# A fused Fourier mixing and feed-forward kernel: transform split 49 by 64 instead of 56 by 56, its first stage on 64x64 tiles of TensorE

## The chip, the cores and the metric

One NeuronCore of one Trainium2 chip runs the whole kernel. The metric is the device time of one execution in microseconds. Times and profiles come from the chip; a profile is one execution taken by the hardware profiler.

## The reference

Two parts follow each other. The first is a Fourier transform over the sequence of 3136, a complex 256 by 256 mixing with bias and a soft threshold, and the inverse transform. The second is a gated feed-forward part with a convolution of three taps.

```python
batch, seq, dim = (8, 3136, 256); d_ff = 1024
X = np.fft.rfft(x, axis=1)
Yr = Xr @ w_r - Xi @ w_i + b_r
Yi = Xr @ w_i + Xi @ w_r + b_i
Yr = np.sign(Yr) * np.maximum(np.abs(Yr) - 0.01, 0.0)      # Yi likewise
y = np.fft.irfft(Yr + 1j * Yi, n=3136, axis=1)
h = np.maximum(y @ w_in, 0.0)
for k in range(3):                                # hp: h with a row of zeros at both ends
    conv_out += conv_w[k][None, None, :] * hp[:, k:k + S, :]
out = h * (1.0 / (1.0 + np.exp(-conv_out))) @ w_out
```

## The kernel before

The transform of length 3136 = 56 x 56 is done in two matmul steps with twiddle factors in the second step's table, and back in two more. Through the middle the data passes twice through DRAM, as `sc1` (after the first step) and `sc2` (after the third).

- **Stage one** (`stage1`, and `stage1_head` for batch 0): a call takes four columns `j` of one batch (`JC = 4`), loads them as `xr` (112 rows: 56 points of two halves), and multiplies with the block-diagonal table `f1` in two plain fp32 matmuls 112x112 by 512 columns. ScalarE copies each result (`ps_s`, one PSUM bank) to `a1`, and one DMA stores it to `sc1`. A batch takes 7 calls; 56 in all.
- **Stage two** (`stage2`): an *item* is one batch and one group of four lines `u` (`UG = 4`, `NG = 7` groups a batch, 56 items). `load_a2` gathers 112 x 4 x 256 from `sc1`; eight plain fp32 matmuls with 128 streamed columns (the table `t2`) put the spectrum, transposed, into `ps_s2`. ScalarE and VectorE split it into a high and a low fp32r part (`fh`, `fl`).
- **Mix** (`mix`): 36 fp32r matmuls of 256 columns into three banks `ps_mx0` to `ps_mx2`. VectorE adds the bias (`p1`, two operations), forms `v` in four operations, and thresholds it with `r` from ScalarE; `sh` and `sl` are its high and low parts, `sl` by GpSimd.
- **Stage three** (`stage3`): 12 fp32r matmuls with the tables `i1_hi`, `i1_lo` into `ps_s3` (two banks), one copy `z1` by ScalarE, one store to `sc2`.
- **Stage four** (`stage4`): inverse first step. A piece loads `z2` from `sc2` and uses its 128-column slices as the stationary operand; the table `i2` (112 columns) streams. Eight plain fp32 matmuls a piece, `NPC = 7` pieces a batch. The result `yh`, `yl` stays in SBUF.
- **Feed-forward** (`up`, `down`): 12 fp32r matmuls of 450 columns and 21 of 256 for each of 224 steps, with the pieces of stage four of a later batch between them.

Plain fp32 matmuls stand in a profile as two records each. The weights of the feed-forward part arrive as float64 bits and are converted by VectorE and ScalarE in the background (`later`), a few operations per item, from the item 3 on.

The order within each engine is set by the Tile scheduler, from the order of the code and its own estimates. In the code the loop over `it` loads `a2` two items ahead, does stage two of item `it`, mix of `it - 1`, stage three of `it - 3`, and calls of stage one as far ahead as the `while` condition lets it. All DMAs are issued on SyncE's queue. The PSUM banks of this part are one for `ps1` (stage one), two for `ps2`, three for `psm`, two for `psa`.

## Time and profile before

| what | value |
|---|---|
| median of 3 runs (lowest, highest) | 1770.43 us (1767.99, 1770.92) |
| the profiled execution | 1769.05 us, span 1767.3 us |
| granted TensorE clock in it | 0.995 |
| TensorE busy | 1731.0 us (98%), 12096 matmul records |
| VectorE busy | 1524.3 us (86%) |
| ScalarE busy | 1229.1 us (70%) |
| GpSimd busy | 134.7 us (8%) |
| DMA | 164.63 MB, mean 93 GB/s |

The share of busy time is a mean over the transform (about the first third) and the feed-forward part, and these have different limits; stretches of the span have to be read apart. The ends of matmul records are modelled, so the distance from one start to the next says what a matmul costs. A line such as L245 names the line of the kernel's code.

### The profile page before, as it was taken

The numbers are of one execution on the slowest core, as the hardware profiler recorded it, in microseconds if no ns is written. First come the engines' busy times: TensorE is split into PE (matmuls) and PEld (weight loads), VectorE is DVE, ScalarE is ACT, GpSimd is POOL, SyncE is SP. The second block draws the span as 40 slices with busy tenths as digits, with TensorE's granted clock in tenths as the row PEclk, the third lists the DMA queues.
The fourth block names the chain that finished last, engine by engine and source line by source line (L and its number), as shares of the span: only waits on it lengthen the run. The fifth ranks groups of instructions, "written<-read, shape, count | busy, mean of one in ns | idle before, by whom it ended". The sixth has DMA issues, their size and how long they took to land.

```text
span 1767.3 us, 29387 instructions
## 1 busy us (share of the span) xinstructions
PE 1731.0 (98%) x12096; PEld 1621.6 (92%) x12096; DVE 1524.3 (86%) x1820; ACT 1229.1 (70%) x1590; POOL 134.7 (8%) x60
## 2 busy tenths in 40 slices
PE   6899999999998999999999999999999999999999
PEld 2788888888998999999999999999999999999998
DVE  2899999998896988988888888888888888888887
ACT  2667777776665777777777777777777777777766
POOL 0122222222232000000000000000000000000000
PEclk8999999999999999999999999999999999999999
DMA  9777677677534110111111011111101111100001
GB/s 263 216 230 236 196 232 216 192 230 228 164 111 136 43 43 22 32 53 53 32 53 53 22 55 51 49 46 52 43 22 43 53 43 43 42 22 22 22 22 42
DMA packets 107382, 164.63 MB, mean 93 GB/s; under 512 B 8816, under 2 KB 86000, under 8 KB 107248
## 3 DMA queue, kind: packets, MB, share of 16 engines
q1 hardware_dynamic: 107248, 162.74, 30.9%
q8 instruction: 96, 1.57, 0.4%
q14 instruction: 38, 0.31, 0.1%
HBM read 85.65 MB, written 77.07 MB: 92 GB/s over the span
## 4 chain that ended last, share of the span: by engine, by line
PE 93%; DMA 3%; DVE 1%; ACT 1%; issue 0%; SPq 0%; ACTq 0%
PE acc L470 31%; PE ps_h L442 31%; PE ps_mx L304 12%; PE ps_s L423 5%; PE ps_s L280 5%; PE ps_s L331 4%; PE ps_s L245 4%; DMA i_raw<-in_inv_dram 2%; DMA z<-sc 1%; DMA sc<-ha 0%; DMA a<-sc 0%; DMA sc<-a 0%; ACT a L246 0%; DVE cw L212 0%; DVE yl L430 0%
## 5 line engine op out<-in xcount | busy, mean ns | idle before, releaser
L470 PE MATMUL acc<-wout,gh 128*128 128x256 f32 x3136 | 567.0, 280 | 0.0
L451 DVE SCALAR_TENSOR_TENSOR c<-h,cw,c 128x896 f32<-128x896 f32 x448 | 513.1, 1147 | 47.3 <-ACT c L449 46.3
L442 PE MATMUL ps_h<-yh,win 128*128 128x450 f32 x1792 | 551.0, 368 | 0.1
L470 PEld LDWEIGHTS acc<-wout,gh 128*128 128x128 f32 x3136 | 493.7, 188 | 6.5
L470 PE MATMUL acc<-wout,gl 128*128 128x256 f32 x1568 | 437.6, 281 | 0.0
L444 ACT ACTIVATE h<-ps_h 128x900 f32<-128x900 f32 x224 | 207.7, 927 | 254.8 <-PE ps_h L442 254.8
L442 PEld LDWEIGHTS ps_h<-yh,win 128*128 128x128 f32 x1792 | 338.7, 189 | 26.4 <-DVE yl L430 0.8
L442 PE MATMUL ps_h<-yl,win 128*128 128x450 f32 x896 | 329.2, 367 | 0.0
L470 PEld LDWEIGHTS acc<-wout,gl 128*128 128x128 f32 x1568 | 293.7, 188 | 0.1
L457 DVE TENSOR_TENSOR gl<-c,gh 128x896 fp32r<-128x896 f32 x224 | 243.1, 1089 | 53.6 <-ACT gh L456 50.1
L453 DVE TENSOR_TENSOR c<-h,c 128x896 f32<-128x896 f32 x224 | 243.6, 1088 | 46.9 <-ACT c L452 46.7
L456 ACT CAST gh<-c 128x896 fp32r<-128x896 f32 x224 | 209.8, 942 | 49.4 <-DVE c L453 49.4
L452 ACT ACTIVATE c<-c 128x896 f32<-128x896 f32 x224 | 213.3, 952 | 23.9 <-DVE c L451 21.0
L304 PE MATMUL ps_mx<-wmix_lo,fh 128*128 128x256 f32 x672 | 202.2, 301 | 0.0
L304 PE MATMUL ps_mx<-wmix_hi,fh 128*128 128x256 f32 x672 | 196.9, 294 | 0.5 <-DVE v L313 0.3
L304 PE MATMUL ps_mx<-wmix_hi,fl 128*128 128x256 f32 x672 | 188.7, 282 | 1.3 <-DVE fl L288 1.2
L442 PEld LDWEIGHTS ps_h<-yl,win 128*128 128x128 f32 x896 | 168.9, 189 | 11.0
L449 ACT ACTIVATE c<-h,cw 128x896 f32<-128x896 f32 x168 | 175.5, 1044 | 2.6 <-DVE gl L457 0.2
L321 POOL TENSOR_TENSOR sl<-v,sh 128x1024 fp32r<-128x1024 f32 x56 | 134.5, 2402 | 423.1 <-PE ps_s L331 300.0
L313 DVE TENSOR_TENSOR v<-ps_mx,p 64x512 f32<-64x512 f32 x224 | 154.0, 688 | 3.3
L304 PEld LDWEIGHTS ps_mx<-wmix_lo,fh 128*128 128x128 f32 x672 | 126.4, 188 | 12.3 <-issue 12.3
L304 PEld LDWEIGHTS ps_mx<-wmix_hi,fl 128*128 128x128 f32 x672 | 126.0, 188 | 11.8 <-issue 9.9
(84 smaller groups left out, 2023.0 us busy)
## 6 DMA issues: line engine op xcount, KB each, us to landing
a<-sc SPq DMA_DIRECT2D x56, 448.0 KB, 5.0
sc<-z SPq DMA_DIRECT2D x56, 448.0 KB, 3.3
z<-sc SPq DMA_DIRECT2D x56, 448.0 KB, 3.8
xr<-in_x_dram SPq DMA_DIRECT2D x55, 448.0 KB, 4.7
out_dram<-o SPq DMA_DIRECT2D x27, 896.0 KB, 4.0
sc<-a SPq DMA_DIRECT2D x49, 448.0 KB, 4.9
sc<-ha SPq DMA_DIRECT2D x7, 448.0 KB, 7.5
win_bits<-in_moe_w_in_dram SPq DMA_DIRECT2D x4, 512.0 KB, 7.6
```

Of the source, the lines that this page charges most:

```text
L304: nc.tensor.matmul(ps[c][:, k, :], lt, rh, start=(n == 0), stop=(n == len(mm) - 1))
L313: nc.vector.tensor_tensor(v[dst, :, k, :], ps[c][src], p1[src, c], op=ALU.add)
L321: SL_ENG.tensor_tensor(sl, v, sh.bitcast(F32), op=ALU.subtract)
L442: nc.tensor.matmul(ps[:, a, 0:CH + 2], lt, rh, start=(n == 0), stop=(n == len(mm) - 1))
L444: nc.scalar.activation(h, ps[:, :, 0:CH + 2], AF.Relu)
L449: nc.scalar.mul(c, h[:, :, 0:CH], cw[:, 0, f:f + 1])
L451: nc.vector.scalar_tensor_tensor(c, h[:, :, k:k + CH], cw[:, k, f:f + 1], c, op0=ALU.mult, op1=ALU.add)
L452: nc.scalar.activation(c, c, AF.Sigmoid)
L453: nc.vector.tensor_tensor(c, h[:, :, 1:CH + 1], c, op=ALU.mult)
L456: nc.scalar.copy(gh, c)
L457: nc.vector.tensor_tensor(gl, c, gh.bitcast(F32), op=ALU.subtract)
L470: nc.tensor.matmul(acc[m // 2][:, m % 2, :], lt[:, sl], rh[:, f, :], start=(f == 0 and n == 0 and m % 2 == 0), stop=(f == NF - 1 and n == ...
```

## The change

The length is split as 49 x 64 instead of 56 x 56. In the first step 49 points give 25 lines `u` (0 to 24; 1 to 24 complex, 0 real), in the second step 64 points give 64 lines of the spectrum.

- **Items.** Lines 1 to 24 are six groups of four per batch. Line 0 of four batches is gathered into one item of its own, twice: 50 items instead of 56. Such an item loads four pieces of 64 rows and stores four pieces.
- **Stage one.** A call again takes four columns `j`, of 64 half-columns (`H = 32`), so a batch takes 8 calls. The two halves lie at partitions 0 to 48 and 64 to 112. `quarters` issues four matmuls with 49 rows and 64 output columns of the array each, streaming 512 columns: two halves times two pairs of columns, each with tile size 64x64 and its own corner of the array. The two halves write two banks. Two loads and two stores a call instead of one and one.
- **Stage three** writes in two halves of two lines, through a single bank, with a copy each. `ps1` now has two banks and `psa` one.
- **Mix.** The two additions of the bias become one of 1024 elements that reads `ps[2]` twice; `r` lies in the memory of `p1`; `sl` has two buffers.
- **Stage four.** `z2` has 100 rows, the streamed table 98 columns; 8 pieces a batch.
- The `while` condition of stage one lets it run ahead by other numbers.

```diff
-R = 56
-U = 28
-SL = 57
+R = 49
+R2 = 64
+U = 24
 SP = 64
-H = 28
+H = 32
...
+NQ = H // 4
...
-        ps1 = ab.enter_context(tc.tile_pool(name="ps1", bufs=1, space=PSUM))
+        ps1 = ab.enter_context(tc.tile_pool(name="ps1", bufs=2, space=PSUM))
...
+        def load_x(pool, b, jc, **kw):
+
+            xr = pool.tile([P, JC, D], F32, name="xr", **kw)
+            xv = x[b].rearrange("(n h j) d -> h n j d", h=2, j=H)
+            for h in range(2):
+                ld = nc.sync.dma_start(xr[h * SP:h * SP + R], xv[h, :, jc * JC:(jc + 1) * JC, :])
             return xr, ld
 
+        def quarters(ps, xr):
+
+            for c in range(2):
+                for h in range(2):
+                    rows = slice(h * SP, h * SP + R)
+                    nc.tensor.matmul(ps[h][c * SP:(c + 1) * SP], f1[rows, :], xr[rows, 2 * c:2 * c + 2, :], start=True, stop=True)
+
+        def store_a1(b, jc, a1):
+
+            for c in range(2):
+                j = jc * JC + 2 * c
+                st = nc.sync.dma_start(sc1[b].rearrange("(w h) j d -> w h j d", h=2)[:, :, j:j + 2, :], a1[c * SP:c * SP + R])
+            return st
+
         def stage1(b, jc):
 
             xr, _ = load_x(s1p, b, jc, bufs=XRB)
-            a1 = s1p.tile([K1, JC, D], F32, name="a1", bufs=2)
-            for j in range(0, JC, 2):
-                ps = ps1.tile([K1, 2, D], F32, name="ps_s1")
-                nc.tensor.matmul(ps, f1, xr[:, j:j + 2, :], start=True, stop=True)
-                nc.scalar.copy(a1[:, j:j + 2, :], ps)
-            return nc.sync.dma_start(sc1[b][:, jc * JC:(jc + 1) * JC, :], a1)
+            a1 = s1p.tile([P, 2, JC // 2, D], F32, name="a1", bufs=2)
+            ps = [ps1.tile([P, JC // 2, D], F32, name="ps_s1") for h in range(2)]
+            quarters(ps, xr)
+            for h in range(2):
+                nc.scalar.copy(a1[:, h], ps[h])
+            return store_a1(b, jc, a1)
...
         def load_a2(b, g):
-            a2 = a2p.tile([K1, UG, D], F32, name="a2")
-            ld = nc.sync.dma_start(a2, sc1[b].rearrange("(u q) j d -> (q j) u d", q=4)[:, g * UG:(g + 1) * UG, :])
+            a2 = a2p.tile([KQ, UG, D], F32, name="a2")
+            if g < NG:
+                rows = slice(g * 4 * UG, (g + 1) * 4 * UG)
+                ld = nc.sync.dma_start(a2, sc1[b][rows].rearrange("(u q) j d -> (q j) u d", q=4))
+            else:
+                for k in range(UG):
+                    ld = nc.sync.dma_start(a2[0:R2, k, :], sc1[b + k][4 * U:K1].rearrange("q j d -> (q j) d"))
             return a2, ld
...
-            for c in range(2):
-                nc.vector.tensor_tensor(p1[:, c], ps[2], bias[:, c], op=ALU.add)
+            nc.vector.tensor_tensor(p1, ps[2].unsqueeze(1).broadcast_to([K2, 2, UG // 2, D]), bias, op=ALU.add)
...
-            sl = wk.tile([K2, UG, D], F32R, name="sl", bufs=1)
-            r = wk.tile([K2, UG, D], F32, name="r", bufs=1)
+            sl = wk.tile([K2, UG, D], F32R, name="sl")
+            r = p1.rearrange("p c k d -> p (c k) d")
...
-            ps = psa.tile([K1, UG, D], F32, name="ps_s3")
-            for k in range(UG):
-                u = g * UG + k
-                for n, (lt, rh) in enumerate(((i1_hi, sh), (i1_hi, sl), (i1_lo, sh))):
-                    nc.tensor.matmul(ps[:, k, :], lt[:, u, :], rh[:, k, :], start=(n == 0), stop=(n == 2))
-            z1 = io.tile([K1, UG, D], F32, name="z1", bufs=2)
-            nc.scalar.copy(z1, ps)
-            nc.sync.dma_start(sc2[b][:, g * UG:(g + 1) * UG, :], z1)
+            z1 = io.tile([KQ, UG, D], F32, name="z1", bufs=2)
+            for c in range(0, UG, 2):
+                ps = psa.tile([KQ, 2, D], F32, name="ps_s3")
+                for k in range(c, c + 2):
+                    u = g * UG + k if g < NG else U + k % 2
+                    for n, (lt, rh) in enumerate(((i1_hi, sh), (i1_hi, sl), (i1_lo, sh))):
+                        nc.tensor.matmul(ps[:, k - c, :], lt[:, u, :], rh[:, k, :], start=(n == 0), stop=(n == 2))
+                nc.scalar.copy(z1[:, c:c + 2, :], ps)
+            if g < NG:
+                nc.sync.dma_start(sc2[b][:, g * UG:(g + 1) * UG, :], z1)
+            else:
+                for k in range(UG):
+                    nc.sync.dma_start(sc2[b + k][:, U, :], z1[:, k, :])
...
-        AHEAD = NG + 3
         items = [(b, g) for b in range(B) for g in range(NG)]
+        for b in (0, UG):
+            items.insert(items.index((b + UG - 1, 0)), (b, NG))
         n_it = len(items)
+        firsts = [(b, jc) for b in range(B) for jc in range(NQ)]
...
-            while p1 < n_it and p1 < min(it + AHEAD, NG + 2 + it + it // 2):
-                stage1(*items[p1])
+            while p1 < min(len(firsts), NQ + 2 + 2 * it, NQ + 5 + 4 * it // 3):
+                stage1(*firsts[p1])
                 p1 += 1
...
-        z2 = zio.tile([K1, JG, D], F32, name="z2")
+        z2 = zio.tile([KI, JG, D], F32, name="z2")
```

How the order of instructions moves shows best at two places. A row of the order is one instruction (or several alike): line, operation, output and inputs by the program's names, shape.

TensorE before, in the middle of the transform, from the end of one item's stage three to the next item's mix (`ps_s_2797` is stage three, `ps_s_2816` stage one, `ps_s_2831` and `ps_s_2840` stage two):

```order
L331 MATMUL ps_s_2797<-sh,i_lo 112x256
L245 MATMUL ps_s_2816<-xr,f_113 112x512
L280 MATMUL ps_s_2831<-t_114,a_2608 128x128 x4
L280 MATMUL ps_s_2840<-t_114,a_2608 128x128 x4
L304 MATMUL ps_mx_2853<-wmix_hi,fh 128x256
```

TensorE now, at the same place (`ps_s_3065` is the first half of a stage three and `ps_s_3073` the second half of the same one, `ps_s_3086` and `ps_s_3087` the two halves of stage one, `ps_s_3104` and `ps_s_3113` stage two):

```order
L352 MATMUL ps_s_3065<-sh,i_lo 128x256
L248 MATMUL ps_s_3086<-xr,f_113 64x512
L248 MATMUL ps_s_3087<-xr,f_113 64x512
L248 MATMUL ps_s_3086<-xr,f_113 64x512
L248 MATMUL ps_s_3087<-xr,f_113 64x512
L300 MATMUL ps_s_3104<-t_114,a_2873 128x128 x4
L300 MATMUL ps_s_3113<-t_114,a_2873 128x128 x3
L352 MATMUL ps_s_3073<-sh,i_hi 128x256
```

The four quarters stand where one matmul of stage one stood (the second one of a call stood among the mix matmuls), and stage three is pulled apart around them and stage two. In 16 of the 54 calls in the loop the quarters are issued as two pairs, one bank each, with mix matmuls between.

VectorE before, from one item's p to its threshold step (`p_3867`; the third and the second row from the end belong to the next item's stage two):

```order
L309 TENSOR_TENSOR p_3867<-ps_mx_3830,bias 128x512 x2
L288 TENSOR_TENSOR fl<-d,fh 128x2x256
L313 TENSOR_TENSOR v<-ps_mx_3828,p_3867 64x2x256 x2
L313 TENSOR_TENSOR v<-ps_mx_3829,p_3867 64x2x256 x2
L285 TENSOR_TENSOR d<-ps_s_3916,d 128x256
L286 TENSOR_TENSOR fl<-ps_s_3916,fh 128x512
L319 SCALAR_TENSOR_TENSOR v<-v,r 128x1024
```

VectorE now, from an item's p to its threshold step, and what follows:

```order
L328 TENSOR_TENSOR p_3753<-ps_mx_3716,bias 128x1024
L305 TENSOR_TENSOR d<-ps_s_3703,d 128x256
L306 TENSOR_TENSOR fl<-ps_s_3703,fh 128x512
L332 TENSOR_TENSOR v<-ps_mx_3714,p_3753 64x2x256 x2
L308 TENSOR_TENSOR fl<-d,fh 128x2x256
L332 TENSOR_TENSOR v<-ps_mx_3715,p_3753 64x2x256 x2
L338 SCALAR_TENSOR_TENSOR v<-v,p_3753 128x1024
L204 TENSOR_TENSOR wout_m<-wout_m,wout_80 128x512
```

The threshold step, which needs ScalarE's `r`, has moved up to the v additions that `r` is made from: directly behind them in 21 of 50 items (before in 9 of 56), with one operation between in 11 (before in 5).

More of the change, by code (lines that the diff above doesn't have):

```diff
@@ L42, in _tables @@
     f[:, 1, :] = -np.sin(ang)
-    f[:, 1, 0] = np.where(n % 2 == 0, 1.0, -1.0)
-    fwd1 = np.zeros((2, R, U, 2, 2))
-    for h in range(2):
-        fwd1[h, :, :, :, h] = f.transpose(0, 2, 1)
+    fwd1 = np.zeros((2, SP, SP))
+    for uu in range(1, U + 1):
+        for c in range(2):
+            fwd1[:, :R, (uu - 1) * 2 + c] = f[:, c, uu]
+    fwd1[:, :R, 2 * U] = f[:, 0, 0]
     g = np.transpose(f, (1, 2, 0)).copy()
@@ L50, in _tables @@
     g /= S
-    inv2 = np.zeros((2, 2 * U, R, 2))
+    g = np.roll(g, -1, axis=1)
+    inv2 = np.zeros((2, 2 * (U + 1), R, 2))
     for i in range(2):
-        inv2[i, :, :, i] = g.reshape(2 * U, R)
-    fwd2 = np.zeros((2, R, U, 2, SP))
-    inv1 = np.zeros((2, SP, U, 2, R))
-    for uu in range(U):
-        for s in range(SL):
+        inv2[i, :, :, i] = g.reshape(2 * (U + 1), R)
+    fwd2 = np.zeros((2, R2, U + 1, 2, SP))
+    inv1 = np.zeros((2, SP, U + 2, 2, R2))
+    for uu in range(U + 1):
+        at = (uu - 1) % (U + 1)
+        for s in range(SP):
+            k = uu + R * s
+            th = 2 * np.pi * ((k * n2) % S) / S
+            sn, cs = np.sin(th), np.cos(th)
@@ new lines, in _tables @@
+                fwd2[0, :, at, 1, s] = -sn
+                inv1[0, s, at, 0, :] = w * cs
+                inv1[1, s, at, 0, :] = -w * sn
+            else:
+                sg = 1.0 if k <= S // 2 else -1.0
+                fwd2[0, :, at, 0, s] = cs
+                fwd2[1, :, at, 0, s] = sn
+                fwd2[0, :, at, 1, s] = -sn * sg
+                fwd2[1, :, at, 1, s] = cs * sg
+                inv1[0, s, at, 0, :] = cs
+                inv1[0, s, at, 1, :] = sn
+                inv1[1, s, at, 0, :] = -sg * sn
+                inv1[1, s, at, 1, :] = sg * cs
@@ L99, in spectral_ffn_kernel @@
     nc = tc.nc
-    K1, K2 = 2 * R, 2 * SP
+    K1, K2, KQ, KI = 2 * R, 2 * SP, 2 * R2, 4 * (U + 1)
     dram = ctx.enter_context(tc.tile_pool(name="dram", bufs=1, space=DRAM))
     sc1 = [dram.tile([K1, H, D], F32, name=f"sc1_{b}") for b in range(B)]
-    sc2 = [dram.tile([K1, U, D], F32, name=f"sc2_{b}") for b in range(B)]
+    sc2 = [dram.tile([KQ, U + 1, D], F32, name=f"sc2_{b}") for b in range(B)]
     cst = ctx.enter_context(tc.tile_pool(name="cst", bufs=1))
-    i2 = cst.tile([K1, K1], F32, name="i2")
+    i2 = cst.tile([KI, 112], F32, name="i2")[:, 0:K1]
     cw = cst.tile([P, 3, NF], F32, name="cw")
@@ L165, in load_inv1 @@
         def load_inv1(g):
-            raw = stg.tile([K2, UG, K1], F32, name="i1_raw", tag="raw", bufs=2)
-            sl = slice(g * UG, (g + 1) * UG)
+            sl = slice(g * UG, min((g + 1) * UG, U + 2))
+            raw = stg.tile([K2, sl.stop - sl.start, KQ], F32, name="i1_raw", tag="raw", bufs=2)
             nc.sync.dma_start(raw, inv1v[:, sl, :])
@@ L252, in stage1_head @@
                 for jc, xr in enumerate(xs):
[L253 to L265 removed]
+                    a1 = ha.tile([P, 2, JC // 2, D], F32, name=f"ha{jc}")
+                    if jc % 2:
+                        ps = [psm.tile([P, JC // 2, D], F32, name="ps_s1h", tag=f"ps_mx{h}") for h in range(2)]
+                    else:
+                        ps = [ps1.tile([P, JC // 2, D], F32, name="ps_s1") for h in range(2)]
+                    quarters(ps, xr)
+                    nc.scalar.copy(a1[:, 0], ps[0])
+                    nc.vector.tensor_copy(a1[:, 1], ps[1])
+                    st = store_a1(b, jc, a1)
             return st
         def load_a2(b, g):
[L269 to L270 removed]
+            a2 = a2p.tile([KQ, UG, D], F32, name="a2")
+            if g < NG:
+                rows = slice(g * 4 * UG, (g + 1) * 4 * UG)
+                ld = nc.sync.dma_start(a2, sc1[b][rows].rearrange("(u q) j d -> (q j) u d", q=4))
+            else:
+                for k in range(UG):
+                    ld = nc.sync.dma_start(a2[0:R2, k, :], sc1[b + k][4 * U:K1].rearrange("q j d -> (q j) d"))
             return a2, ld
@@ L279, in stage2 @@
                 for k in range(UG):
-                    nc.tensor.matmul(ps[:, k], a2[:, k, t * P:(t + 1) * P], t2[:, g * UG + k, :],
+                    rows, u = (KQ, g * UG + k) if g < NG else (R2, U)
+                    nc.tensor.matmul(ps[:, k], a2[0:rows, k, t * P:(t + 1) * P], t2[0:rows, u, :],
                                      start=(k == 0), stop=(k == UG - 1), skip_group_check=True)
@@ L348, in spectral_ffn_kernel @@
             xh = []
-            for p in range(NG):
-                xr, ld = load_x(hx, 0, p, parts=2 if p == 0 else 1, tag=f"hx{p}")
+            for p in range(NQ):
+                xr, ld = load_x(hx, 0, p, tag=f"hx{p}")
                 xh.append(xr)
```

83 lines of the change are left out of this document (26 added, 57 removed).

## The prediction

> **What bounds the kernel now.** I read the table of stretches first, since the busy shares of the page are means over two different programs (the transform, up to 548 us, and the feed-forward part), and then the timeline of TensorE inside each.
>
> ```profile
> core 0: us, PE busy (x) PEld busy (x) DVE busy (x) ACT busy (x) POOL busy (x), PEclk, DMA share, GB/s
> 33.00:146.00 113.00, 103.91 (x711) 87.95 (x710) 94.79 (x163) 70.64 (x122) 21.99 (x9) 0.97 0.82 231
> 146.00:480.00 334.00, 334.00 (x2491) 298.08 (x2490) 309.05 (x497) 236.43 (x380) 86.14 (x37) 1.00 0.70 208
> 480.00:548.00 68.00, 65.21 (x558) 64.59 (x556) 66.44 (x108) 45.59 (x68) 21.64 (x9) 1.00 0.37 109
> 548.00:612.00 64.00, 59.59 (x409) 56.38 (x410) 46.30 (x49) 42.49 (x44) 4.75 (x2) 0.97 0.40 109
> 612.00:1750.00 1138.00, 1138.00 (x7798) 1095.63 (x7797) 989.67 (x983) 819.39 (x958) 0.00 (x0) 1.00 0.13 39
> ```
>
> From 146 to 480 us TensorE is busy all the time (334.00 of 334), VectorE for 309. From 480 to 548 the order turns: VectorE 66.44 of 68. From 612 on TensorE bounds alone. So a cut in TensorE's work counts in the first stretch only until VectorE is reached, and any TensorE work added behind 612 counts in full.
>
> The timeline of TensorE gives one item (one pass of stage two, mix and stage three) with stage one in it, and one without:
>
> ```profile
> start us, us, engine line op out<-in xcount [idle before <-releaser]
> 159.85 1.02 PE L245 MATMUL ps_s<-xr,f 112*112 112x512 f32 x2
> 160.71 1.95 PE L280 MATMUL ps_s<-t,a 112*128 112x128 f32 x16
> 162.41 0.37 PE L304 MATMUL ps_mx<-wmix_hi,fh 128*128 128x256 f32 x1
> 162.62 0.28 PE L304 MATMUL ps_mx<-wmix_lo,fh 128*128 128x256 f32 x1
> 162.73 0.28 PE L304 MATMUL ps_mx<-wmix_hi,fl 128*128 128x256 f32 x1
> 168.98 1.02 PE L245 MATMUL ps_s<-xr,f 112*112 112x512 f32 x2
> ...
> 486.99 1.95 PE L280 MATMUL ps_s<-t,a 112*128 112x128 f32 x16
> 494.41 1.95 PE L280 MATMUL ps_s<-t,a 112*128 112x128 f32 x16
> ```
>
> The ends are modelled, so I use starts. One plain fp32 matmul of stage one leaves two records and takes 160.71 - 159.85 = 0.86 us, 0.43 a record; the eight of stage two take 1.70. The item repeats every 168.98 - 159.85 = 9.13 us, without stage one every 494.41 - 486.99 = 7.42. The difference, 1.71, is two stage-one matmuls.
>
> VectorE without and with the weight conversion that runs beside it:
>
> ```profile
> 510.21 2.81 DVE L313 TENSOR_TENSOR v<-ps_mx,p 64x512 f32<-64x512 f32 x4
> 514.92 1.28 DVE L309 TENSOR_TENSOR p<-ps_mx,bias 128x512 f32<-128x512 f32 x2
> 516.12 1.22 DVE L319 SCALAR_TENSOR_TENSOR v<-v,r 128x1024 f32<-128x1024 f32 x1
> 517.25 0.68 DVE L288 TENSOR_TENSOR fl<-d,fh 128x512 fp32r<-128x512 f32 x1
> 517.86 2.81 DVE L313 TENSOR_TENSOR v<-ps_mx,p 64x512 f32<-64x512 f32 x4
> ...
> 301.98 0.69 DVE L188 SCALAR_TENSOR_TENSOR wout_e<-wout_bits,wout_e 128x512 int32<-128x512 int32 x1
> 302.58 0.42 DVE L189 TENSOR_SCALAR wout_m<-wout_bits 128x512 int32<-128x512 int32 x1
> 302.91 1.28 DVE L309 TENSOR_TENSOR p<-ps_mx,bias 128x512 f32<-128x512 f32 x2
> ```
>
> Back to back VectorE needs 517.86 - 510.21 = 7.65 us an item. Conversion steps take 0.60 or 0.33 each: five of the one and three of the other in each of eight pieces, 8 x 4.0 = 32 us, with some 2 for the small table 34 us.
>
> **The change, part by part.** Times are in us, against the profiled execution of 1769.05 (span 1767.3), which is 1.4 under the median of 1770.43.
>
> *Six items fewer.* 56 become 50: 48 and two for the lines u = 0 of four batches each. TensorE: 6 x 7.42 = -44.5. Their DMAs move nothing that TensorE waits for in the table.
>
> *Stage one in quarters.* Eight calls a batch instead of seven. The loop before holds 47 calls of 1.72; now it holds 54 (64 less eight of the head and two ahead of the loop), in its first 40 items, 1.35 each. A call is now four matmuls on 64x64 tiles, each still 512 columns and, as plain fp32, two records of 0.43. No row shows two matmuls side by side. Low end: four tiles at once, the two records of a tile behind each other, 0.86. High end: eight records in a row, 3.44. In the program's order 38 calls have the four quarters together and 16 are cut by mix matmuls into two pairs; at the low end pairs cost 2 x 0.86, so the mean is (38 x 0.86 + 16 x 1.72) / 54 = 1.11. Each of some 1.33 uninterrupted pieces per call enters and leaves the small tiles. The nearest row for such a seam is the step from stage two to mix, 162.41 to 162.62, 0.21 where the next step takes 0.11: 0.1 lost. With a weight load in the open at both ends it would be 2 x 0.19, by
>
> ```profile
> L280 PEld LDWEIGHTS ps_s<-t,a 112*128 112x128 f32 x896 | 109.9, 194 | 26.0 <-issue 12.1 <-PE ps_s L331 9.7 <-DMA a<-sc 4.2
> L245 PE MATMUL ps_s<-xr,f 112*112 112x512 f32 x196 | 102.1, 602 | 16.6 <-DMA xr<-in_x_dram 10.6 <-ACT a L246 6.0
> ```
>
> I take 0.25 a piece, 0.33 a call: X = 1.11 + 0.33 = 1.44 a call, bounds 1.1 and 3.8. I stay near the low end because quarters share neither rows and columns nor, across rows, a bank; it is a choice, and the largest uncertainty here.
>
> A rule that speaks against it: the Trainium skill, "TensorEngine Tiling (Array Packing)", Key Properties, says that a change of tiling mode drains TensorE. No run here has a change of mode; by it the seam is a real cost on both sides of every piece, nearer to 0.4 than to 0.1, and the sum below would be 54 x 1.33 x 0.15 = 11 us longer.
>
> *Stage three in halves.* The same 12 matmuls. The second half needs the one bank that ScalarE must first empty; between the halves the order puts the quarters and seven of stage two's eight matmuls, over 2.3 us, against a half copy near 0.6.
>
> ```profile
> ACT z L333 <- PE ps_s L331: 74.7, 43, 3.1
> DVE v L319 <- ACT r L318: 16.2, 18, 1.6
> ...
> L246 ACT COPY a<-ps_s 112x512 f32<-112x512 f32 x98 | 58.3, 595 | 19.7 <-PE ps_s L245 18.4 <-DMA sc<-a 0.4
> L333 ACT COPY z<-ps_s 112x1024 f32<-112x1024 f32 x56 | 56.7, 1013 | 78.8 <-PE ps_s L331 74.7 <-DMA sc<-a 4.0
> ```
>
> ScalarE waits for TensorE there (74.7 us), not the reverse; two copies of 0.6 for one of 1.01 add 0.2 an item to an engine busy 236 of 334. Cost 0 while that cover stands. Were a half copy late by its own length each time, 50 x 0.6 = 30 us.
>
> *VectorE.* The two p additions become one of 1024 elements: 1.20 to about 1.14 (the step from L319 to L288), so 7.6 an item; a gain of 3 in all. r now lies in p's place, and the threshold step must follow before the next p. In the new order it stands directly behind the v additions in 21 of 50 items, with one short operation between in 11 (before: 9 and 5 of 56). The 16.2 us of that wait lay mostly on these 14, about 1.2 each; now 21 x 1.2 + 11 x 0.5 = 31, or 0.6 an item. With conversion, 34 / 40 = 0.85: 7.6 + 0.6 + 0.85 = 9.05 us for an item of the first 40. The second sl buffer takes a wait from GpSimd, which nobody waits for: 0.
>
> *DMA.* Four issues an item become about seven, at 0.32 us of SyncE each:
>
> ```profile
> 308.86 0.32 SPq L270 DMA_DIRECT2D a<-sc  x1
> ```
>
> That is 2.2 of 9.5 us; the bytes stay the same, and the stretch runs at a DMA share of 0.70. 0, unless the queue stands behind one late store.
>
> *Stage four.* Eight pieces a batch for seven, each eight matmuls of 98 columns instead of 112.
>
> ```profile
> 617.92 1.94 PE L423 MATMUL ps_s<-i,z 112*128 112x112 f32 x16
> 619.63 0.36 PE L470 MATMUL acc<-wout,gl 128*128 128x256 f32 x1
> ...
> 569.20 2.01 PE L423 MATMUL ps_s<-i,z 112*128 112x112 f32 x16 [1.24 <-DMA z<-sc]
> 572.29 2.01 PE L423 MATMUL ps_s<-i,z 112*128 112x112 f32 x16 [1.09 <-DMA z<-sc]
> ```
>
> 16 records take 619.63 - 617.92 = 1.71, as much as stage two's 16 with 128 columns (1.70). So the columns streamed don't set this; the 128 weight columns, which stay, do. Seven pieces more behind 574 us: 7 x 1.71 = 12; batch 0's extra piece falls where pieces come at 572.29 - 569.20 = 3.1 with their loads: 3. Together +15. Had the columns set the time, it would be 0.
>
> *Sum.* First 40 items: TensorE 7.42 + 1.35 x 1.44 = 9.36, VectorE 9.05; with two engines so close I add 0.15: 9.5 x 40 = 380. Last ten: VectorE 7.6 + 0.5 = 8.1: 81. The first 113 us hold about 10.3 items (56 less 334 / 9.13 and less nine behind 480), so the start costs 113 - 94 = 19 over the steady rate; kept. 480 us against 515 (548 - 33): -35. With stage four -35 + 15 = -20: 1749 against 1769.05, 1750 beside the median.
>
> **Rivals.** *A: the quarters overlap* (the forecast). X from 1.1 to 1.75: with 1.1 VectorE bounds at 9.05, 368 + 81 + 19 = 468, 1738; with 1.75, 9.8 x 40 gives 492, 1762.
>
> *B: records go strictly in turn.* A quarter's second record has to follow its first on the same tile, 0.43 later, as in L245's rows. If TensorE starts no matmul before the one ahead in the program has started, the next quarter waits behind that second record, and only a second record and the next first one overlap: 5 x 0.43 = 2.15 for four quarters, 2 x 3 x 0.43 = 2.58 for two pairs, 2.28 in the mean, 2.4 to 2.6 with seams. An item then takes 7.42 + 1.35 x 2.45 = 10.7: 428 + 81 + 19 = 528, +13 + 15 = +28: 1797 (1785 to 1806). For it: 112-row records here do start strictly one behind the other. Against: all of them use the same tile. It ends on the other side; the point that decides is X = 1.93, where 40 x (7.42 + 1.35 X) + 100 + 15 = 515. The Trainium skill says so in "TensorE: Matmul & The Clock Gate", Part 3: matmuls start and end in program order, different tiles some 4 ns apart. No run here shows it yet.
>
> *C: no overlap at all.* X = 3.44 to 3.8: 12.3 x 40 + 100 = 592, +77 + 15: 1861.
>
> *D: the saving is there but VectorE's waits eat it*, 0.4 an item more than I count: 1769, no change. For it: VectorE is busy for 309 of 334 us already.
>
> **Chances.** A 0.47, B 0.34, C 0.09, D 0.05, other 0.05. About 0.2% (3.5 us) is what a measurement of this kernel can tell from no change. Faster: nearly all of A, a little of B: 0.50; the same: D and the edges of A and B: 0.08; slower: 0.42. The forecast is A's 1750, its own range 1733 to 1764. The range takes in most of B, 1730 to 1803, and leaves out C and the tails.
>
> **What would show it.** Starts of the quarters' records: four tiles within 0.1 us of each other and the group done in 0.9 to 1.2 is A; starts 0.43 apart in pairs is B; eight steps of 0.43 is C. The item should last about 9.5 us while stage one runs and 8.1 after it, with VectorE busy over 95%; TensorE idle and VectorE's wait for r well over 31 us would be D. Stage four's 16 records should still take 1.71. I am wrong first of all if X lies above 1.93.

## The result and the profile after

The changed kernel takes 1797.3 us (median of 4 runs, 1792.33 to 1802.17), the kernel before 1770.68 on the same chip: a ratio of 1.0151 (95% interval 1.0116 to 1.0187). It is slower by 27 us; 1750 were forecast. The profiled execution took 1802.17 us, span 1800.4, the slowest of the four. The four go with their granted clock (1792.33 and 1794.28 us at 0.991 and 0.994, 1800.33 and 1802.17 at 0.985 and 0.981), so the +33.1 of the profiled one in the table of stages below is more than the 27 of the medians.

The part that the prediction held for its largest uncertainty, the quarters, cost about what was forecast. TensorE's timeline in the middle of the transform, first the group of four quarters and what follows, then two narrower windows inside the group:

```profile
271.88 1.09 PE L248 MATMUL ps_s<-xr,f 49*64 49x512 f32 x8
272.90 0.49 PE L300 MATMUL ps_s<-t,a 128*128 128x128 f32 x2
...
271.88 0.66 PE L248 MATMUL ps_s<-xr,f 49*64 49x512 f32 x4
...
272.37 0.61 PE L248 MATMUL ps_s<-xr,f 49*64 49x512 f32 x4
```

Eight records begin at 271.88 and the next matmul follows 1.02 us later. The first four records start together (7 ns apart in the trace), and the second four together, 0.48 us on. A pair of quarters takes 1.01 as well. A piece of stage four behaves as forecast too:

```profile
671.24 1.92 PE L449 MATMUL ps_s<-i,z 100*128 100x98 f32 x16
672.95 0.48 PE L496 MATMUL acc<-wout,gh 128*128 128x256 f32 x2
```

Sixteen records take 672.95 - 671.24 = 1.71 us with 98 columns, as with 112 before.

The stretches of the profile answer to the table of before (which showed 231 GB/s, a DMA share of 0.82 and TensorE busy for 103.91 in its first row):

```profile
core 0: us, PE busy (x) PEld busy (x) DVE busy (x) ACT busy (x) POOL busy (x), PEclk, DMA share, GB/s
33.00:146.00 113.00, 90.41 (x531) 61.63 (x524) 61.88 (x103) 52.01 (x98) 13.38 (x6) 0.89 0.62 201
185.68:476.12 290.44, 278.38 (x2159) 229.76 (x2158) 261.94 (x375) 196.20 (x351) 69.67 (x29) 0.99 0.65 222
493.64:541.00 47.36, 47.15 (x400) 46.32 (x399) 46.02 (x68) 33.03 (x57) 14.33 (x6) 1.00 0.35 123
548.00:612.00 64.00, 58.95 (x337) 56.93 (x336) 35.42 (x42) 31.45 (x37) 7.07 (x3) 0.73 0.34 104
```

The second row holds 29 items: 10.0 us each, where 9.5 were forecast, and TensorE, never idle there before, now stands still for 12 us. Counted from threshold step to threshold step, the two profiled executions differ like this (us):

| stage | before | after | difference | forecast |
|---|---|---|---|---|
| start of the span to first threshold step | 60.0 | 82.8 | +22.7 | 0 |
| first to last threshold step | 490.2 | 481.9 | -8.4 | -35 |
| last threshold step to first matmul of the feed-forward part | 23.8 | 28.0 | +4.2 | +3 |
| feed-forward part with stage four | 1193.2 | 1207.7 | +14.5 | +12 |
| sum | 1767.3 | 1800.4 | +33.1 | -20 |

So two terms are missing: the start, and about three quarters of the saving in the items. Both have their rows. SyncE's queue at the start (timeline) of the kernel before:

```profile
1.18 4.32 SPq L236 DMA_DIRECT2D xr<-in_x_dram  x8
16.80 7.76 SPq L265 DMA_DIRECT2D sc<-ha  x7
```

The same of the changed kernel:

```profile
1.20 11.95 SPq L240 DMA_DIRECT2D xr<-in_x_dram  x16
23.66 19.07 SPq L254 DMA_DIRECT2D sc<-ha  x16
```

Batch 0's loads are issued over 11.95 us instead of 4.32, its stores over 19.07 instead of 7.76. VectorE inside the loop, timeline of the changed kernel:

```profile
301.13 2.81 DVE L332 TENSOR_TENSOR v<-ps_mx,p 64x512 f32<-64x512 f32 x4
305.21 1.23 DVE L338 SCALAR_TENSOR_TENSOR v<-v,p 128x1024 f32<-128x1024 f32 x1 [1.28 <-ACT p L337]
```

Its waits in the 29 items (us in total, times, longest):

```profile
DVE v L338 <- ACT p L337: 25.3, 27, 1.3
```

And two of its groups there (busy us and mean ns of one):

```profile
L308 DVE TENSOR_TENSOR fl<-d,fh 128x512 fp32r<-128x512 f32 x29 | 23.1, 796 | 0.5
L205 DVE TENSOR_TENSOR wout<-wout_m,wout_rest 128x512 fp32r<-128x512 f32 x4 | 7.7, 1923 | 0.0
```

(`p` in L337 and L338 is r, which lies in p's memory.) VectorE waits 1.28 us for r behind nearly every item's v, 25.3 in all or 0.87 an item. The conversion step L205, 0.69 a time before, takes 1.92 on average. Busy 261.94 and waiting 25.3 make 9.90 of the 10.0 us of an item.

### The profile page after: what moved, and what is told of

It reads as the page before. It is cut to its first block, busy times and chain, and to the rows that moved or that the text cites. A ratio compares the mean times of both kernels' runs of the same rounds, so it can differ in the third digit from the quotient of the medians.

```text
span 1800.4 us, 29326 instructions
## 1 busy us (share of the span) xinstructions
PE 1737.4 (97%) x12128; PEld 1596.2 (89%) x12128; DVE 1489.8 (83%) x1707; ACT 1203.6 (67%) x1615; POOL 119.9 (7%) x54
## 3 DMA queue, kind: packets, MB, share of 16 engines
q1 hardware_dynamic: 114654, 163.89, 27.4%
## 4 chain that ended last, share of the span: by engine, by line
PE 82%; DVE 8%; DMA 5%; issue 2%; ACT 2%; SPq 1%; ACTq 0%; DVEq 0%
PE ps_h L468 31%; PE acc L496 31%; PE ps_s L449 7%; PE ps_mx L324 7%; DVE v L332 3%; PE ps_s L300 3%; PE ps_s L352 3%; PE ps_s L248 2%; DMA xr<-in_x_dram 2%; DVE fl L306 1%; DVE p L328 1%; ACT p L337 1%; DMA sc<-a 1%; DMA sc<-z 1%; DVE d L305 1%
## 5 line engine op out<-in xcount | busy, mean ns | idle before, releaser
L496 PEld LDWEIGHTS acc<-wout,gh 128*128 128x128 f32 x3136 | 490.2, 188 | 5.1
L324 PE MATMUL ps_mx<-wmix_hi,fh 128*128 128x256 f32 x600 | 173.8, 291 | 0.8 <-ACT fh L304 0.5
L324 PE MATMUL ps_mx<-wmix_hi,fl 128*128 128x256 f32 x600 | 169.5, 285 | 3.2 <-DVE fl L308 3.1
L324 PE MATMUL ps_mx<-wmix_lo,fh 128*128 128x256 f32 x600 | 170.4, 285 | 0.0
L340 POOL TENSOR_TENSOR sl<-v,sh 128x1024 fp32r<-128x1024 f32 x50 | 119.7, 2394 | 452.3 <-ACT sh L339 326.7
L300 PEld LDWEIGHTS ps_s<-t,a 128*128 128x128 f32 (+1 forms) x800 | 100.8, 198 | 47.0 <-issue 10.1
L332 DVE TENSOR_TENSOR v<-ps_mx,p 64x512 f32<-64x512 f32 x200 | 137.4, 687 | 5.6 <-PE ps_mx L324 1.2
L449 PEld LDWEIGHTS ps_s<-i,z 100*128 100x128 f32 x1024 | 133.3, 205 | 1.6
```

The lines of the kernel that those rows point to most:

```text
L324: nc.tensor.matmul(ps[c][:, k, :], lt, rh, start=(n == 0), stop=(n == len(mm) - 1))
L332: nc.vector.tensor_tensor(v[dst, :, k, :], ps[c][src], p1[src, c], op=ALU.add)
L449: nc.tensor.matmul(ps[:, t, j * K1:(j + 1) * K1], z2[:, j, t * P:(t + 1) * P], i2, start=(j == 0), stop=(j == JG - 1), skip_group_check=True)
L496: nc.tensor.matmul(acc[m // 2][:, m % 2, :], lt[:, sl], rh[:, f, :], start=(f == 0 and n == 0 and m % 2 == 0), stop=(f == NF - 1 and n == ...
```

## The experiments

### Three tries on the changed kernel

**r without its wait.** r gets memory of its own and is made from the constant bias instead of v, so the threshold is another:

```diff
-            r = p1.rearrange("p c k d -> p (c k) d")
-            nc.scalar.activation(r, v, AF.Relu, bias=mlam)
+            r = wk.tile([K2, UG, D], F32, name="r", bufs=1)
+            nc.scalar.activation(r, bias.rearrange("p c k d -> p (c k) d"), AF.Relu, bias=mlam)
```

> Leaves out the dependence of the threshold on v: r lies in memory of its own and is made from the constant bias, with the same ScalarE instruction, so that VectorE's threshold step never waits for it. Theory 'VectorE in turn' (the loop of items is bound by VectorE's own work of 9.0 us an item plus 0.87 us of waiting for r): the wait of the threshold step goes from 36 us to below 5, an item between 185 and 476 us takes 9.2 to 9.5 us instead of 10.0, the run 25 to 35 us less than the changed kernel's 1797, about 1767. Rival 'TensorE's seams' (the small tiles and the split third stage cost TensorE the time): the wait goes, but the item stays at 9.9 and the run within 8 us of 1797.

1816.23 us, ratio 1.0266 (1.0235 to 1.0297): slower, a miss for every theory. The wait for r is gone, but other waits stand in its place; of ScalarE's waits from 191 to 476 us the largest in total is for stores of stage one:

```profile
ACT a L264 <- DMA sc<-a: 30.5, 13, 5.2
```

**One sl buffer again.** `sl = wk.tile(..., bufs=1)`.

> Undoes one part: sl has one buffer again. Theory 'collision': with two buffers GpSimd makes sl right behind sh, where VectorE's conversion steps run, and these last up to 1.9 us instead of 0.69; with one buffer GpSimd is back behind stage three, the conversion steps are all 0.69 again, some 12 us less VectorE work, the run 5 to 12 us below 1797. Rival 'the second buffer is needed': stage three then holds sl over both halves, mix waits, the run is 5 to 20 us above 1797.

1829.37 us, 1.0336 (1.0318 to 1.0353). Both theories had expected at most 20 us of change; the direction is that of the rival. The second buffer, which the prediction priced at nothing, is worth 32 us here; items 9 to 39 take 10.5 us each instead of 10.0.

**The start.** First the mixing weight's VectorE steps are put behind the copies of stage one; then, besides, every second load and store of batch 0 goes through ScalarE's queue.

```diff
-                load_mix()
+                raw = load_mix()
                 load_bias()
                 st = stage1_head(xh)
+                finish_mix(raw)
```

> The splitting of the mixing weights is issued behind stage one of batch 0 instead of ahead of it, so VectorE's copies of stage one no longer stand behind a load that lands at 25.7 us. Theory 'queue' (SyncE's queue sets the start: 16 loads in 12 us and 16 stores in 19 us, where the kernel before had 8 in 4.3 and 7 in 7.8): the stores still begin at about 23.7 us and end at 42 to 43, the first threshold step stays within 3 us of 82.8, the run within 4 us of 1797. Rival 'VectorE blocks the head': the stores end 10 us earlier, the first threshold step comes at 70 to 73 us, the run at about 1786.

> As the run before it (mixing weights split later), and in the head every second load and every second store is issued by ScalarE instead of SyncE, so that two queues carry them. Theory 'queue': the stores of the head end at 28 to 33 us instead of 42.7, the first threshold step comes at 66 to 72 us instead of 82.8, the run 10 to 16 us below 1797, about 1784. Rival 'the transfers themselves are the limit' (49 rows at a time): the two queues share the same rate, the first threshold step stays at 80 or later, the run within 4 us of 1797.

1801.68 us (1.0171, 1.0144 to 1.0197) and 1799.1 us (1.0154, 1.0128 to 1.018). The first threshold steps come at 84.9 and 80.8; at item 9 both versions stand where the changed kernel stands. Neither the order nor the issuing queue holds the start back. The DMA share stayed at 0.45 with two queues issuing.

### The transfers of 49 rows

Five versions change how the rows of stage one's loads and stores are cut into transfers; the matmuls stay. In the changed kernel: 48 rows each, and the two odd rows of both halves in one more transfer; 128 rows in one transfer, whose pattern has the two halves as its first dimension; 64 rows in each of two. The last two move 30% more bytes. In the kernel before: its 112 rows cut into 49 and 63, and into 56 and 56.

```diff
-                ld = nc.sync.dma_start(xr[h * SP:h * SP + R], xv[h, :, jc * JC:(jc + 1) * JC, :])
+                nc.sync.dma_start(xr[h * SP:h * SP + R - 1], xv[h, 0:R - 1, cols, :])
+            ld = nc.sync.dma_start(xr[R - 1::SP], xv[:, R - 1, cols, :])
...
-                ld = nc.sync.dma_start(xr[:, k:k + w, :], xv[:, k:k + w, :])
+                for q in (slice(0, 49), slice(49, K1)):
+                    ld = nc.sync.dma_start(xr[q, k:k + w, :], xv[q, k:k + w, :])
```

> The changed kernel; each transfer of 49 rows is made one of 48 rows, and the two odd rows (48 of both halves) go together in one more transfer. Bytes and matmuls stay. Theory 'seven engines' (in the trace of the changed kernel exactly 7 packets are in flight while 49-row transfers run, 16 in the kernel before; 49 = 7 x 7, 48 = 3 x 16): 15 to 16 packets in flight at the start, first threshold step at 62 to 67 us instead of 82.8, items 3 to 9 at about 10 us instead of 11.4, total 1762 to 1780. Rival 'more and smaller transfers' (16 loads and 16 stores of 196 KB at the start instead of 8 and 7 of 448): still more issues now, first threshold at 80 or later, total 1797 or more. Rival 'mutual waits of the engines pace the loop': the start is quicker by up to 20 us, but items stay at 10 and catch nothing up; 1780 to 1795.

> The changed kernel; a call of stage one loads and stores 128 rows in one transfer each (64 a half, of which 49 are used; the last batch's loads stay at 49 rows). 30% more bytes in these transfers, but two issues a call instead of four. Theory 'seven engines': 16 packets in flight, first threshold at 64 to 70, total 1765 to 1785, a little behind the 48-row version if bytes count, ahead of it if issues do. Rival 'more bytes or smaller packets are the limit': as slow as the changed kernel or slower, 1797 to 1810.

> The kernel before; each 112-row load and store of stage one goes as one of 49 and one of 63 rows. Matmuls and bytes stay. Theory 'seven engines' (49 rows on 7, 63 on 9): 7 to 9 packets in flight at the start instead of 16, first threshold 15 to 25 us later, total 1785 to 1800. Rival 'the number of issues': as the split in 56 and 56 rows, both slower by the same 5 to 15 us. Rival 'neither': 1771.

> The kernel before; each 112-row load and store of stage one goes as two of 56 rows: the same issues as in the split by 49 and 63, but rows that divide by 14. Theory 'seven engines': 14 packets in flight, first threshold within 4 us of the kernel before, total 1769 to 1776. Rival 'the number of issues': slower by 5 to 15 us, and as slow as the split by 49 and 63.

> The changed kernel; each transfer of 49 rows is made one of 64 rows (the last batch's loads stay at 49), four issues a call as in the changed kernel, 30% more bytes in them. Theory 'engines by the first dimension of the transfer' (49 rows on 7, 48 rows on 16, and where the first dimension was the two halves, on 2): 16 packets in flight, first threshold at 62 to 68, total 1772 to 1785, like the 48-row version. Rival 'the bytes bound by then': DMA share over 0.9 in the loop and total over 1790.

| version | us | ratio to before (interval) | first threshold step | DMA share, 7 to 11 us |
|---|---|---|---|---|
| kernel before | 1769.18 | | 60.0 | 1.04 |
| changed kernel | 1797.3 | 1.0151 (1.0116 to 1.0187) | 82.8 | 0.45 |
| 48 rows and the odd ones | 1780.77 | 1.0064 (1.0043 to 1.0085) | 65.2 | 0.99 |
| 64 rows | 1780.85 | 1.0047 (1.0029 to 1.0065) | 69.8 | 1.04 |
| 128 rows, halves first | 2697.57 | 1.5263 (1.5232 to 1.5295) | | 0.13 |
| before, 49 and 63 | 1795.31 | 1.0153 (1.0134 to 1.0172) | 81.2 | 0.57 |
| before, 56 and 56 | 1771.89 | 1.0014 (1.0004 to 1.0024) | 62.1 | 0.88 |

Each ratio is to the kernel before as it ran beside that version; 1769.18 us is its median beside the versions with 48 and 128 rows and its own two. The last column is from the table of stretches, while batch 0 is loaded (the row's last three numbers are clock, DMA share and GB/s). The kernel before:

```profile
7.00:11.00 4.00, 3.50 (x5) 1.07 (x4) 0.69 (x1) 0.47 (x1) 0.00 (x0) 1.00 1.04 283
```

The changed kernel:

```profile
7.00:11.00 4.00, 4.00 (x18) 1.14 (x16) 1.22 (x2) 0.80 (x2) 0.00 (x0) 1.00 0.45 172
```

The changed kernel with 48 rows:

```profile
7.00:11.00 4.00, 3.96 (x20) 0.82 (x16) 1.38 (x2) 1.17 (x2) 0.00 (x0) 1.00 0.99 238
```

The kernel before by 49 and 63 rows:

```profile
7.00:11.00 4.00, 2.92 (x3) 0.90 (x4) 0.69 (x1) 0.36 (x1) 0.00 (x0) 1.00 0.57 201
```

The shares are sixteenths: 7/16 = 0.44 for 49 rows, 9/16 = 0.56 behind 63, 14/16 = 0.88 for 56, all for 48, 64 and 112, and 2/16 = 0.13 where the first dimension was 2. The packets in flight most of this time in the trace's DMA records are 7, 9, 14, 16 and 2. The rate falls less than the share: seven engines moved 172 GB/s, sixteen 283. The kernel before, cut by 49 and 63, comes to its first threshold step nearly as late as the changed kernel (81.2 and 82.8); cut by 56 and 56, with the same number of issues, it loses almost nothing. And 64 rows with 30% more bytes are as good as 48, so bytes are not the limit either. The version with 128 rows, expected at 1765 to 1785, missed by far, as its pattern began with a dimension of 2. This cause of the late start is shown; taking it out of the changed kernel gives back 16.5 us (1797.3 to 1780.8).

### VectorE's loop

With 48 rows the items still take 9.99 us (items 9 to 39). Two runs on that base: VectorE's conversion work left out, and the conversion steps moved between v and the threshold step.

```diff
+            with tc.issue_after(last.ins):
+                for _ in range(steps):
+                    last = next(background, None) or last
+            with tc.issue_after(last.ins):
+                thr = nc.vector.scalar_tensor_tensor(v, v, LAM, r, op0=ALU.add, op1=ALU.min)
```

> The version with 48-row transfers; VectorE's part of the weight conversion in the transform is left out (seven operations for each of eight pieces; ScalarE copies the raw high words instead, so that ScalarE's count stays), so the weights of the feed-forward part are others. Theory 'VectorE bounds the item' (busy 9.0 of 10.0 us, 0.87 of waiting for r behind v, and conversion steps that run 1.3 to 2.3 us instead of 0.4 to 0.7 while GpSimd forms sl): items 9 to 38 fall from 9.97 to 9.3 to 9.5, where TensorE bounds at 9.36; total 1755 to 1766. Rival 'ScalarE's queue (58 us of standing at r for v, fh behind it) paces TensorE': VectorE's load does not matter, items at 9.8 or more, total 1772 or more.

> The version with 48-row transfers; the two or three conversion steps of an item are put between the v additions and the threshold step instead of behind the threshold step, so that they run while VectorE waits for r, and ahead of GpSimd's sl instead of beside it. Work stays the same. In the program the threshold step then stands directly behind v in 1 of 50 items instead of 21. Theory 'VectorE bounds the item by its waits': the wait for r falls from 0.87 an item to under 0.2 and the stretched steps disappear (0.4 an item), items 9 to 38 at 9.3 to 9.5, total 1757 to 1768, faster than the kernel before. Rival 'ScalarE's queue paces': r is as late as before relative to v, items at 9.8 or more, 1773 or more. Rival 'later sl': sl comes 1.2 us later and stage three waits for it; 1780 or more.

Without conversion 1788.13 us (1.0092, 1.0062 to 1.0123), no faster than with it: the theory's number missed. The granted clock was 0.96 in this stretch, but that is not the reason: of the items 9 to 38, the 21 that ran wholly at full clock took 10.0 us each as well. With the fill 1768.99 us (0.9983, 0.9965 to 1.0001), 12 us less with the same work. Without conversion the items take 10.1 us, with the fill 9.63. Stretch of 29 items without conversion:

```profile
177.81:472.00 294.19, 287.76 (x2172) 238.82 (x2172) 244.56 (x323) 190.58 (x340) 72.13 (x29) 0.96 0.72 210
```

VectorE's longest wait in it:

```profile
DVE v L345 <- ACT p L344: 37.3, 29, 1.6
```

Stretch of 29 items with the fill:

```profile
175.07:453.66 278.59, 273.26 (x2146) 226.82 (x2146) 261.70 (x374) 197.24 (x353) 69.34 (x29) 1.00 0.75 226
```

The wait for r in it:

```profile
DVE v L345 <- ACT p L340: 5.4, 11, 1.3
```

Taking work away did not help, since the order moved with it: the threshold step then stood directly behind v in 36 of 50 items, the wait for r grew from 24.5 to 37.3 us, and fl took 1.37 us instead of 0.82. Putting work into the gap helped: the wait fell to 5.4 us. The step L205 is back at 0.69, but fl takes 1.03, so VectorE's busy time is nearly what it was (261.70 us against 262.81 with 48 rows alone): the gain is the wait. What counts here is not VectorE's load but what stands between v and the threshold step, and beside what.

The second half of that, beside what a step runs, was settled on the kernel before, with the change's smaller parts alone: all of them (one bias step, r in p's memory, second sl, stage three in halves), r in p's memory only, the halves only, and the halves with GpSimd's sl left out.

```diff
-            ps = psa.tile([K1, UG, D], F32, name="ps_s3")
+            for c in range(0, UG, 2):
+                ps = psa.tile([K1, 2, D], F32, name="ps_s3")
...
-            sl = wk.tile([K2, UG, D], F32R, name="sl", bufs=1)
-            SL_ENG.tensor_tensor(sl, v, sh.bitcast(F32), op=ALU.subtract)
+            sl = sh
```

> The kernel before with the change's smaller parts alone: one bias step of 1024 elements, r in p's memory, a second sl, stage three in halves with one bank each (the second bank stays unused). No new split, no quarters. If these parts make the waits by themselves: TensorE idle appears in its items (0 of 291 us before), 1780 or more. If the waits come only with the shorter TensorE time of the new split and its order: items stay at 9.13, total 1768 to 1774.

> The kernel before with one edit: r lies in p's memory. Nothing is computed otherwise. If this is the part that costs: items of 9.6 to 9.9 instead of 9.13, total 1788 to 1800, and VectorE always either busy or at the wait for r late in the loop. If stage three in halves is the part: 1768 to 1774.

> The kernel before with one edit: stage three in two halves, each in one bank and with its own copy (one of the two banks stays unused). If r in p's memory is the part that costs: 1766 to 1774, TensorE without idle time from 190 to 480. If the halves cost (waits of stage three for ScalarE's copy of the first half, 4.7 us in 218 where all parts were together): 1780 or more.

> The kernel before with stage three in halves, and GpSimd's sl left out (stage three takes sh in its place, the same number of matmuls, so the low part's share of the result is wrong). If GpSimd's operation beside VectorE's is what makes the halves dear: VectorE's busy time per item falls from 9.8 to 8.6, its steps on SBUF all take 0.7, items back at 9.1 to 9.3, total 1765 to 1778. If the halves' own waits for ScalarE's copies do it: items at 9.8 or more, 1800 or more.

| the kernel before with | us | ratio (interval) |
|---|---|---|
| all smaller parts | 1797.34 | 1.0163 (1.0149 to 1.0178) |
| r in p's memory | 1775.29 | 1.0022 (1.0013 to 1.0031) |
| stage three in halves | 1813.6 | 1.0246 (1.0232 to 1.026) |
| halves, no sl on GpSimd | 1767.74 | 0.9984 (0.9972 to 0.9997) |

With all parts VectorE repeats every 9.90 us in the last items with stage one, always busy or waiting (timeline, first and third row an item apart):

```profile
446.70 1.23 DVE L318 SCALAR_TENSOR_TENSOR v<-v,p 128x1024 f32<-128x1024 f32 x1 [1.28 <-ACT p L317]
...
450.96 1.64 DVE L288 TENSOR_TENSOR fl<-d,fh 128x512 fp32r<-128x512 f32 x1
...
456.60 1.22 DVE L318 SCALAR_TENSOR_TENSOR v<-v,p 128x1024 f32<-128x1024 f32 x1 [1.28 <-ACT p L317]
```

It is the pattern of the changed kernel: 1.28 us of waiting for r, and fl at 1.64 instead of 0.69. I had expected r in p's memory to be the dear part; it costs 4 to 5 us, and the halves, which the prediction priced at 0, cost 43. GpSimd at one place of the kernel before with halves:

```profile
324.79 3.10 POOL L321 TENSOR_TENSOR sl<-v,sh 128x1024 fp32r<-128x1024 f32 x1 [8.52 <-PE ps_s L333]
```

VectorE at the same place:

```profile
324.45 1.22 DVE L319 SCALAR_TENSOR_TENSOR v<-v,r 128x1024 f32<-128x1024 f32 x1
325.58 2.85 DVE L188 SCALAR_TENSOR_TENSOR wout_e<-wout_bits,wout_e 128x512 int32<-128x512 int32 x1
```

The stretch from 191 to 480 with halves:

```profile
191.00:480.00 289.00, 272.01 (x1957) 236.87 (x1956) 282.27 (x392) 188.01 (x328) 78.19 (x29) 0.99 0.67 197
```

TensorE's largest wait in it is for fl, one of the lengthened steps:

```profile
PE ps_mx L304 <- DVE fl L288: 13.8, 14, 1.8
```

The same stretch with halves and without sl:

```profile
191.00:480.00 289.00, 289.00 (x2160) 258.29 (x2159) 264.99 (x427) 204.56 (x358) 0.00 (x0) 1.00 0.69 207
```

GpSimd starts sl at 324.79, when stage three's last matmul has let go of the one sl buffer. The conversion step that VectorE starts at 325.58 takes 2.85 us instead of 0.69: it ends at 328.43, 0.54 us after GpSimd (327.89). In this stretch VectorE is busy for 282.27 of 289 and TensorE idle for 17, of which 13.8 are the wait for fl. With GpSimd's operation out, VectorE's busy time falls to 264.99, TensorE is busy all the time and the kernel is back at its old time. Stretched are only steps whose inputs all lie in SBUF; v, p and d, which read PSUM too, take their 0.69, 0.68 and 0.42 beside sl as elsewhere. In the kernel before sl fell beside v: over 100 of the 127 v steps in this stretch run next to GpSimd, at 0.69. Taking sl out also moved the threshold step nearer to v, so a part of the 46 us between the two runs could be the order; for the wait for r that order was worse, though: 12.2 us without sl, none with it.

All parts together cost less than the halves alone. The likely reason is the second sl buffer: from 191 to 476 us GpSimd's wait ends with sh in 24 of 30 cases, with the halves alone with stage three in 24 of 28. The halves with the second buffer and nothing else were not run. In the changed kernel with one buffer the stretched steps come to 31 us in 285 (each against the median of its kind clear of GpSimd), with two buffers to 12 in 290.

### Whether the two causes add, and a version that beats both

The changed kernel with the fill and its 49 rows; then the 48-row version with the fill and both edits of the start; then the same with r in its own memory.

> The changed kernel with its 49-row transfers, and the conversion steps between v and the threshold step. If the two causes add up: 1797 less 12 = 1785 (1780 to 1790), items 9 to 38 at 9.6. If the 49-row transfers (DMA share 0.7 at half the engines) pace the loop as soon as the waits are shorter: no gain, 1793 or more, items at 9.9 or more.

> The version with 48-row transfers and the fill; at the start half of batch 0's loads and stores go through ScalarE's queue, and VectorE's steps for the mixing weight stand behind the copies of stage one. With 49-row transfers the same two edits moved nothing at item 9. If the queue's issues and the wait for wm_raw are the 6 us by which the start is still late: first threshold at 58 to 62 instead of 66.4, total 1760 to 1766, faster than the kernel before. If not (bytes, or the loads of the tables): first threshold at 65 or later, 1767 to 1771.

> The version with 48-row transfers, fill and the two edits of the start, and r in memory of its own. If r in p's memory still binds VectorE's order there: items 9 to 38 from 9.62 to 9.3 to 9.5, total 1756 to 1764, faster than the kernel before beyond its measurement. If TensorE (9.4 an item) and the program's order are what is left: no change, 1765 to 1770.

| version | us | ratio (interval) |
|---|---|---|
| 49 rows, fill | 1795.51 | 1.0149 (1.0132 to 1.0166) |
| 48 rows, fill | 1768.99 | 0.9983 (0.9965 to 1.0001) |
| 48 rows, fill, start | 1768.42 | 0.9983 (0.9966 to 1.0) |
| 48 rows, fill, start, r own | 1766.79 | 0.998 (0.9971 to 0.9989) |

With 49 rows the fill gains nothing: items stay at 10.05 us, and among ScalarE's waits from 176 to 480 us are 30.5 us for stores (with 48 rows and the fill 0.5 in 29 items):

```profile
ACT a L264 <- DMA sc<-a: 19.0, 9, 3.7
ACT z L357 <- DMA sc<-z: 11.5, 6, 3.4
```

So in the changed kernel the transfers and VectorE's loop each hold an item at about 10 us, and the larger of the two counts, not their sum; the fill could gain its 12 us only after the transfers. The rate does not tell them apart: both versions with the fill move some 225 GB/s in the loop, and the kernel before, cut by 49 and 63, keeps its 9.1 us an item at 220. What differs is the wait for single stores; why they land late was not tried. The edits of the start miss: first threshold step 65.7 against 66.4. The median of the last version lies 0.2% under the kernel before, about as little as can be measured, but this is not shown to come from r: its items still take 9.6 us. All eleven of its executions had a granted clock of 0.993 or more (1763.42 to 1768.61 us). Of the version without r's own memory five of twelve had 0.991 to 0.995, and these took 1760.06 to 1761.73; the other seven, at 0.981 to 0.987, took 1767.97 to 1773.06.

## Why the prediction was wrong

The quarters and stage four came out near their terms. What failed is the term for the transfers, put at 0, and VectorE's time for an item, put at 9.05 us and measured at 9.90.

**Right: the quarters overlap.** X was put at 1.44 us; 38 calls of 1.02 and 16 of 2.02 give 1.32, and the way into the small tiles adds 0.14 a call (48-row version, steps from start to start), so some 1.45. That the sum is so near is luck: the group was put at 0.86 and takes 1.02, and the seams were put at 0.33 a call. The seam is thus not the longer one of the rule that the prediction set against itself (0.2 more a call). Case A's mechanism holds and B is refuted: second records do not keep the next quarter back. That the measured 1797 is just the time that B forecast is chance. The rule of the Trainium skill, "TensorE: Matmul & The Clock Gate", Part 3, fits for the first records (7 ns apart, the page has some 4), but not if both records of a plain fp32 matmul must precede the next matmul. **Right: stage four**, 1.71 a piece; the feed-forward part with it +14.5 for +12, all behind the items +18.7 for +15.

**Wrong: "DMA. ... 0, unless the queue stands behind one late store".** The step counted issues and bytes. It did not ask over how many of the 16 engines a transfer of 49 rows is spread: 7. That is +22.7 at the start, where "kept" stood, and a second limit of 10 us an item in the loop; transfers of 49 and 63 rows alone cost the kernel before 26 us. The Trainium skill states the rule, in "DMA: Bandwidth & Descriptors", "Why a DMA increments its semaphore by 16 and not by 1": the largest number up to 16 that divides the size of the slowest dimension on both sides of the transfer. All seven sizes run here agree. I had not brought it to the change, and the row of before could not show it, as 112 divides by 16.

**Wrong: "VectorE ... 9.05 us for an item".** Measured 9.03 busy and 0.87 waiting, 0.85 more in all. The wait for r was priced at 0.6, 0.27 short. The busy time of 8.45 (7.6 + 0.85) left out the steps stretched beside GpSimd, 12 us in 29 items or 0.42 each; the rest, 0.16, is unexplained. With both, VectorE and not TensorE set the item, 9.9 for 9.36. The forecast's rival D named this mechanism with 0.4 an item and got one chance in twenty.

**Wrong: two edits "at nothing".** For stage three in halves I asked whether TensorE would wait for ScalarE's copy. The cost came through a third engine: the halves move the moment at which GpSimd may start. No run takes the halves out of the changed kernel, so what they cost there is open. For the second sl buffer I wrote that nobody waits for GpSimd. VectorE does, without any semaphore: the list of waits does not show it, only the longer duration of its steps. The rule is in the Trainium skill, "SBUF — State Buffer", "SBUF: two separate sides": GpSimd and VectorE steps with two SBUF inputs, or in a mode that takes both ports, hold one pair of ports in turn. The 0.69 that become 2.85 agree with it.

With both repaired (48 rows, fill) the kernel's terms are +6.4 at the start, -24.3 for the items, +17.6 behind them: -0.3 in the profile against before. The 20 us still missing to the forecast are the start (6), the items (11; 9.6 us each instead of 9.5, and slower ones at the beginning), and 3 behind them.

What stays open: why r without its wait was slower by 19 us than the changed kernel (the late stores are seen, not tried with 48 rows), and what the passage from the transform to the feed-forward part costs. Its granted clock differs between profiles: 0.73 from 548 to 612 us after, 0.97 before; after, it is 0.50 for 34 us from 562.9 on.

## What to carry to other kernels

When a change alters the number of rows of a transfer, divide: the rows' largest divisor up to 16 is the number of engines that carried it in every version here, and sending an odd row apart can be cheaper than keeping it with the others. When an edit moves an operation on GpSimd, look at which VectorE steps will stand beside it, since those that read only SBUF can stand still until it ends, and no wait is shown. And on an engine that waits in order, place work into a known wait before taking work off: here the same steps put ahead of the threshold step instead of behind it gained 12 us, and leaving them out gained nothing.

## What the runs showed of the hardware

- Plain fp32 matmuls on four different 64x64 tiles run side by side with both of their records: eight in 1.02 us, first records 7 ns apart, second records 0.48 us later. Two of them take the same 1.01.
- The engines that carry a transfer follow the first dimension of its pattern: 49 on 7, 56 on 14, 63 on 9, 48, 64 and 112 on 16, and 2 on 2 even where 128 rows follow inside. The last cost half the kernel's time again (2697.57 us).
- Beside a GpSimd operation of 2.4 to 3.1 us a VectorE step on SBUF alone takes up to 2.85 us for 0.69 (steps with one input too: up to 2.60 for 0.42), a step that reads PSUM its usual time.
- Between the transform and the feed-forward part the granted clock is half for a long time in some executions and a short one in others: from 530 to 580 us the mean is 0.66 in the profile of the 48-row version with the fill (0.50 for 34 us), 0.90 in the one with the edits of the start (0.50 for 10 us). In the same places the way from the last threshold step to the feed-forward part took 27.4 and 20.0 us. Nothing was tried on it.
